# Two query blocks in one stretch of 64x64 tiles, with scores and transposed scores in one PSUM tile

## The chip, the cores and the metric

The kernel runs on one core of one Trainium2 chip. The metric is the device time of one execution in microseconds (us), and less is better. Before the change it is 850.53 us, the median of 3 runs (850.13 to 851.92).

Five engines work side by side, each through a list of its own in order: TensorE (PE, matrix products into PSUM, weights loaded by PEld), VectorE (DVE), ScalarE (ACT), GpSimd (POOL) and SyncE (SP), which here only starts transfers. An engine that meets a wait stands still, and all that is queued behind on it stands still too.

## The reference

```python
B, S, D = 1, 2048, 640;  H = 32; Dh = 20; W = 256;  F = 1536
xn = _layernorm(x)
qkv = (xn @ wqkv).reshape(B, S, 3, H, Dh)            # q, k, v: B H S Dh
scores = einsum("bhqd,bhkd->bhqk", q, k) * Dh ** -0.5
mask = (i - j >= 0) & (i - j < W)                     # i query, j key
p = softmax(where(mask, scores, -1e9))
s = einsum("bhqk,bhkd->bhqd", p, v) -> B S D  @ wo
h = relu(xn @ w1 + b1) ** 2;  g = silu(h @ w2 + b2)
return x + s * g
```

A query sees itself and the 255 keys before it. So a block of 128 queries needs three blocks of 128 keys.

## The kernel before

All big products are made with fp16 operands split into a high and a low part, in three products each (high by high, high by low, low by high).

**Ahead of the loop** the kernel goes through 16 tiles of 128 rows: normalize, turn the tile in five transposes (`tps`, line 256), copy it out as a high part on ACT (line 261) and a low part on DVE (line 266), and multiply by the value weights in two groups of 15 matmuls (`vps`, line 292, by `value_tile`). Each group is taken out of PSUM by ACT (line 305) and twice by DVE (line 307). Before the last four tiles stand eight groups of query and key products (`qkps`, line 503).

**The loop over heads** works on pairs of heads, 16 pairs by 16 blocks of 128 queries, so 256 steps and 13 more to run out. At step s the kernel issues, in order:
- when four blocks are complete, the transpose of their maxima (line 583, into a corner of a score tile), whose rows are copied (`mrow`, line 587) and sent by DMA into the query tile `qs`, where they become extra rows of the contraction;
- the scores of block s (`sps`, line 557): four matmuls of 64 queries by 320 keys, two heads by two halves, in the array's 64x64 tiles;
- ten steps behind (`LAG`), the transposed scores (`stps`, line 604), keys by queries, from which the maxima are now subtracted by the extra rows;
- the maxima of both heads under the mask (line 568, DVE; its accumulator is read out in an instruction of its own), and in every fourth step their split into two fp16 numbers on POOL (`mp`, lines 573 and 574);
- the exponentials (line 609, ACT), and on POOL the two masks (lines 610 and 612);
- a step behind, the high part `ph` of the probabilities on ACT (line 617), and two behind the low part `pl` on DVE (line 623);
- in every second step, the products with the values for two blocks (`ops`, line 637); per four blocks they are copied out (`osb`, line 644), summed and divided (lines 648 to 653) and stored.

Between these, `fill` spreads other products evenly over the steps, the filler: the remaining query and key products (15 matmuls of 512 columns), the MLP's first layer (`hps`, 15 of 256 columns) and its second (`yps`, 36 of 320 columns). Each filler group has its evacuation queued in `pending`, issued by `flush`: for `hps` two ACT passes (`relu`, square), a DVE square and a POOL subtraction, for `yps` one DVE pass (line 886).

**After the loop** comes the output stage: transposes `otp` of the attention's result, groups of 15 matmuls by `wo` (`wops`), and a DVE product and sum per group (lines 983 and 984).

The order on each engine is the order in which the code issues, since the loop stands under `manual_schedule`; the framework adds the waits between instructions that touch the same tile. PSUM has eight banks of 512 fp32 columns. Before, they are separate tiles: three for groups (`pmm`: `vps`, `qkps`, `hps`, `yps`, `wops`), two for scores (`pat`), two in one tile for the transposed scores and `tps` (`pst`), one for the values (`po_`).

Of the kernel before, what the change touches and what calls it, by code (L numbers as in the profile page):

```python
# [34 lines left out]
LAG = 10  # L35
PB = 6
# [3 lines left out]
EARLY_FILL = 0.35  # L40
SWING = 0.3
# [16 lines left out]
def attn_mlp_kernel(ctx: ExitStack, tc, x, wqkv, wo, w1, b1, w2, b2, out):  # L58
# [156 lines left out]
    with tc.tile_pool(name="ph1v", bufs=4) as p1v, tc.tile_pool(name="ph1", bufs=2) as p1, tc.tile_pool(name="ph1x", bufs=4) as p1b, tc.tile_pool(name="ph1w", bufs=1) as p1w:  # L215
        xts, xns, mvs, rstds, turns, vts = {}, {}, {}, {}, {}, {}
        wv = [p1w.tile([P, KC, D], F16, name=f"wv{p}") for p in range(2)]
        sums = po_.tile([P, 64], F32, tag="o", name="sums")
# [28 lines left out]
        def turn(i):  # L247
            if i >= NT:
                return
            b, t = divmod(i, 4)  # L250
            if t == 0:
                xT[b] = big(f"xT_{b}", F16).rearrange("p (s c n) -> p s c n", s=2, c=KC)
            ps = pst.tile([P, 2, 4 * P], F32, tag="st", name="tps").rearrange("p a n -> p (a n)")[:, :D].rearrange("p (c n) -> p c n", n=P)
            xn = xns.pop(i)
            for c in range(KC):
                nc.tensor.transpose(ps[:, c, :], xn[:, c * P:(c + 1) * P], ident)
            turns[i] = (ps, [xT[b][:, part, :, t * P:(t + 1) * P] for part in range(2)])
# [37 lines left out]
        def v_bank(i, nh):  # L295
# [3 lines left out]
            return pmm.tile([P, HALF], F32, tag="mm", name="vps")  # L299
# [33 lines left out]
        with tc.manual_schedule(engines={E_.PE, E_.Activation, E_.DVE, E_.Pool, E_.SP}):  # L333
            warm = p1.tile([P, 1], F32, tag="warm", name="warm")
            nc.scalar.activation(warm, eps, AF.Sqrt)
            warm_ps = pmm.tile([P, P], F32, tag="mm", name="warm_ps")
# [155 lines left out]
            for b in range(NB):  # L492
                for w in "kq":
                    hi, lo = ws0[w]
                    ps = pmm.tile([P, BT], F32, tag="mm", name="qkps")
# [49 lines left out]
    mts = {}  # L545

    def scores(p, q, between):
        i = p % 2
        r = [pat.tile([P, 4 * P], F32, tag="s", name="sps") for h in range(2)]
        rows = between and between(r[0])  # L550
        nk = min(WIN + HB, (q + 1) * P)
        for j in range(2):
            q0 = q * P + j * HB
            k0 = max(0, q0 - WIN)
            for h, ps in enumerate(r):
                rows_ = slice(HB * h, HB * h + HR)
                nc.tensor.matmul(ps[HB * j:HB * (j + 1), :nk], qs[i][rows_, q0:q0 + HB], ks[i][rows_, k0:k0 + nk], start=True, stop=True)  # L557
        return (r, mask if q > 1 else mask0[:, 2 * P - nk:], nk), rows

    def maxima(p, q, r):  # L560
        if q % 4 == 0:
            mts[p, q // 4] = mtp_.tile([P, 8], F32, tag="mt", name="mt")
        mt = mts[p, q // 4]
        r, mk, nk = r
        for h, ps in enumerate(r):
            junk = mtp_.tile([P, WIN + HB], BF16, tag="junk", name="junk")
            at_ = 4 * h + q % 4
            nc.vector.tensor_tensor_reduce(out=junk[:, :nk], in0=ps[:, :nk], in1=mk, scale=1.0 / MAX_UNIT, scalar=-3.0e38, op0=ALU.add, op1=ALU.max, accum_out=mt[:, at_:at_ + 1])  # L568
        if q % 4 == 3:
            mp = mps[q // 4 % 2]  # L570
# [6 lines left out]
    def max_rows(p, g, tp=None):  # L577
        i = p % 2
        mp = mts.pop((p, g))
        if tp is None:  # L580
            tp = pat.tile([P, 4 * P], F32, tag="s", name="mtp")
        tp = tp[:, 3 * P:3 * P + P // 2].bitcast(F16)
# [9 lines left out]
    pts = {}  # L592
    ots = {}
    sts = []

    def scores_t(p, kb):
        i = p % 2
        n = min(3, NT - kb) * P
        ps = sts[0]
        for j in range(2):  # L600
            c0, c1 = HB * j, min(n, WIN + HB * (j + 1))
            for hh in range(2):
                rows_ = slice(HB * hh, HB * hh + ER)
                nc.tensor.matmul(ps[HB * j:HB * (j + 1), hh, c0:c1], ks[i][rows_, kb * P + HB * j:kb * P + HB * (j + 1)], qs[i][rows_, kb * P + c0:kb * P + c1], start=True, stop=True)  # L604
        return ps, n

    def exps(p, kb, ps, n):
        p32 = at2.tile([P, 2, 3 * P], F32, tag="p32", bufs=3, name="p32")
        nc.scalar.activation(p32[:, :, :n], ps[:, :, :n], AF.Exp, scale=esc[0], bias=ebias)  # L609
        nc.gpsimd.affine_select(p32[:, :, 0:P], p32[:, :, 0:P], pattern=[[0, 2], [1, P]], compare_op=ALU.is_ge, fill=0.0, base=0, channel_multiplier=-1)  # L610
        if n == 3 * P:
            nc.gpsimd.affine_select(p32[:, :, 2 * P:], p32[:, :, 2 * P:], pattern=[[0, 2], [-1, P]], compare_op=ALU.is_gt, fill=0.0, base=0, channel_multiplier=1)  # L612
        return p32

    def high(p, kb, p32, n):
        ph = at4.tile([P, 2, 3 * P], F16, tag="ph", name="ph")
        nc.scalar.activation(ph[:, :, :n], p32[:, :, :n], AF.Copy)  # L617
        phs[p, kb] = (ph, p32, n)

    def low(p, kb):  # L620
        ph, p32, n = phs.pop((p, kb))
        pl = at4.tile([P, 2, 3 * P], F16, tag="pl", bufs=PB - 1, name="pl")
        nc.vector.tensor_sub(pl[:, :, :n], p32[:, :, :n], ph[:, :, :n])  # L623
        pts[p, kb] = (ph, pl)

    def values(p, q):
        if q % 4 == 0:
            ots[p, q // 4] = po_.tile([P, 4, 2, VW], F32, tag="o", name="ops")
        ot = ots[p, q // 4]
        vp = vps[p]  # L630
        ksr = list(range(max(0, q - 2), q + 1))
        for hh in range(2):
            m = 0
            for k in ksr:
                for t in pts[p, k]:
                    m += 1
                    nc.tensor.matmul(ot[:, q % 4, hh, :], t[:, hh, (q - k) * P:(q - k + 1) * P], vp[:, k // 4, k % 4, hh, :], start=m == 1, stop=m == 2 * len(ksr))  # L637
        if q >= 2:
            del pts[p, q - 2]

    def normed(p, g):
        ot = ots.pop((p, g))
        osb = at2.tile([P, 8, VW], F32, tag="osb", name="osb")
        nc.scalar.activation(osb, ot.rearrange("p a h w -> p (a h) w"), AF.Copy)

        def rest():
            rs = at2.tile([P, 8], F32, tag="rs", name="rs")
            nc.vector.reciprocal(rs, osb[:, :, VW - 1])
            on = at2.tile([P, 8, DH], F32, tag="on", name="on")
            nc.gpsimd.tensor_add(on, osb[:, :, 0:DH], osb[:, :, DH:2 * DH])  # L650

            def last():
                nc.gpsimd.tensor_mul(on, on, rs.unsqueeze(2).to_broadcast([P, 8, DH]))
                post(o_d[g].rearrange("t p d -> p t d")[:, :, 2 * DH * p:2 * DH * (p + 1)], on.rearrange("p (t h) d -> p t (h d)", t=4))
            norm.append(last)
        return rest


    early = at2.tile([P, 1], F32, tag="early", bufs=1, name="early")
    state = [0.0, 0.0, 0]  # L660
# [10 lines left out]
    pending, late = [], []  # L671
# [5 lines left out]
    def flush(upto=None):  # L677
        for f in late[:]:
            f()
        late.clear()  # L680
        while pending and (upto is None or flushed[0] < upto):
            flushed[0] += 1
            pending.pop(0)()

# [32 lines left out]
    AGE = 2  # L717
# [65 lines left out]
    def second_scales():  # L783
        s2, i2 = weight_scale("w2", totals("w2_t", pmm.tile([P, NF], F32, tag="mm", name="sums2"), mlp["g2"]))
# [220 lines left out]
    with tc.manual_schedule(engines={E_.PE, E_.Activation, E_.DVE, E_.Pool, E_.SP}):  # L1005
# [5 lines left out]
        for s in range(steps):  # L1011
# [30 lines left out]
            if b:  # L1042
                stp = scores_t(*b)
# [56 lines left out]
```

## Time and profile before

| | |
|---|---|
| median of 3 runs | 850.53 us (850.13 to 851.92) |
| the profiled execution | 848.83 us, its span 847.0 us |
| PE busy | 822.7 us, 97% of the span |
| DVE busy | 692.8 us, 82% |
| ACT busy | 648.1 us, 77% |
| POOL busy | 485.0 us, 57% |
| granted TensorE clock, mean | 0.998 |

The span goes from the first to the last instruction of the profiled execution. A busy time is the sum of an engine's instructions; the line that the page gives for a group of instructions has its busy time, the mean of one in ns, and the idle time of the engine just before them with what ended it. The list in order of time gives start, length, engine, line, operation and tile. PE's matmuls run one into the other, so their single lengths overlap their neighbours, and the pitch of a run of them says more than the length of one.

### The profile page before, as it was taken

What the parts mean: (1) busy time and instruction counts of PE and PEld (TensorE: products, weight loads), DVE (VectorE), ACT (ScalarE), POOL (GpSimd) and SP (SyncE); (2) the same over time, 40 slices, a digit from 0 to 9 for tenths busy, and PEclk for the clock granted to TensorE, in tenths of its full rate; (3) what the DMA queues carried; (4) which work ended last, traced back from release to release, by engine and by line L of the source; (5) the groups of instructions that cost most, each with busy time, mean ns of one, the idle gap of its engine ahead of it and who ended that gap; (6) DMA issues with size and microseconds to landing.
All of it is one profiled execution on the core that took longest, in us unless ns stands there. A gap on an engine that the chain in (4) does not pass through costs nothing.

```text
span 847.0 us, 25061 instructions
## 1 busy us (share of the span) xinstructions
PE 822.7 (97%) x9426; PEld 553.4 (65%) x9426; DVE 692.8 (82%) x1897; ACT 648.1 (77%) x1028; POOL 485.0 (57%) x874
## 2 busy tenths in 40 slices
PE   8999998999999999999999999999999999999998
PEld 7765553444444676776766766766767767767775
DVE  6776566788999998898988998888988888975655
ACT  5565446998898997897997997987987988993321
POOL 2000001456665798796896986886986977961000
PEclk9999999999999999999999999999999999999999
DMA  7994349755475311213111222113122113055883
GB/s 245 250 349 129 135 127 283 234 162 157 127 229 163 111 44 55 66 33 89 51 49 50 65 52 65 50 33 84 30 76 65 49 42 99 11 180 171 301 297 126
DMA packets 100498, 104.52 MB, mean 123 GB/s; under 512 B 42520, under 2 KB 72856, under 8 KB 100376
## 3 DMA queue, kind: packets, MB, share of 16 engines
q1 hardware_dynamic: 100376, 102.91, 39.8%
q8 instruction: 74, 1.21, 0.6%
q14 instruction: 48, 0.39, 0.2%
HBM read 65.67 MB, written 36.83 MB: 121 GB/s over the span
## 4 chain that ended last, share of the span: by engine, by line
PE 60%; ACT 14%; POOL 8%; DVE 7%; issue 6%; DMA 3%; SPq 1%; DVEq 0%; ACTq 0%; POOLq 0%
PE yps L882 17%; PE wops L688 8%; PE vps L292 7%; PE hps L688 6%; ACT p L609 5%; PE ops L637 5%; PE qkps L688 5%; PE sps L557 4%; ACT ph L617 3%; PE qkps L503 3%; DVE junk L568 3%; PE stps L604 2%; POOL hh L859 2%; DVE pl L623 2%; ACT relu L855 2%
## 5 line engine op out<-in xcount | busy, mean ns | idle before, releaser
L609 ACT ACTIVATE p<-stps,ebias,esc 128x768 f32<-128x768 f32 (+2 forms) x256 | 242.1, 946 | 59.7 <-PE stps L604 48.9
L568 DVE CUSTOM_DVE_ANT_0 junk<-sps,mask 128x320 bf16<-128x320 f32 (+2 forms) x512 | 220.8, 468 | 49.0 <-PE sps L557 41.4
L623 DVE TENSOR_TENSOR pl<-p,ph 128x768 f16<-128x768 f32 (+2 forms) x256 | 248.8, 972 | 3.8 <-ACT ph L617 3.2
L610 POOL TENSOR_SCALAR_AFFINE_SELECT p<-p 128x256 f32<-128x256 f32 x256 | 163.8, 640 | 86.0 <-ACT p L609 76.7
L617 ACT ACTIVATE ph<-p 128x768 f16<-128x768 f32 (+2 forms) x256 | 203.1, 793 | 2.4 <-POOL p L612 1.6
L688 PE MATMUL hps<-xT,w 128*128 128x256 f16 x1440 | 176.2, 273 | 0.0
L882 PE MATMUL yps<-w,hh 128*128 128x320 f16 x1152 | 174.6, 300 | 0.0
L688 PEld LDWEIGHTS <-w 128*128 128x128 f16 x1440 | 132.6, 98 | 36.0 <-issue 17.2
L882 PEld LDWEIGHTS <-hh 128*128 128x128 f16 x1152 | 104.7, 98 | 57.0 <-issue 18.1
L688 PE MATMUL qkps<-xT,qkw 128*128 128x512 f16 x480 | 115.4, 380 | 0.5 <-DVE w_t L153 0.5
L612 POOL TENSOR_SCALAR_AFFINE_SELECT p<-p 128x256 f32<-128x256 f32 x224 | 103.6, 463 | 0.0
L557 PE MATMUL sps<-ks,qs 60*64 60x320 f16 (+2 forms) x1024 | 87.4, 312 | 6.8 <-DVE mt L568 5.9
L637 PE MATMUL ops<-vp,ph 128*128 128x41 f16 x1440 | 89.8, 181 | 0.0
L637 PE MATMUL ops<-vp,pl 128*128 128x41 f16 x1440 | 89.5, 180 | 0.0
L637 PEld LDWEIGHTS <-ph 128*128 128x128 f16 x1440 | 84.5, 96 | 6.2 <-issue 0.6
L604 PE MATMUL stps<-qs,ks 62*64 62x320 f16 (+4 forms) x1024 | 80.9, 293 | 6.7 <-ACT p L609 6.1
L573 POOL CAST mp<-mt 128x8 f16<-128x8 f32 x64 | 44.6, 698 | 70.0 <-DVE mt L568 69.7
L637 PEld LDWEIGHTS <-pl 128*128 128x128 f16 x1440 | 78.9, 96 | 5.6
L859 POOL TENSOR_TENSOR hh<-sq,hh 128x256 f16<-128x256 f32 x96 | 74.9, 782 | 6.4 <-DVE sq L858 4.3
L688 PEld LDWEIGHTS <-qkw 128*128 128x128 f16 x480 | 41.6, 98 | 55.4 <-issue 11.7
L292 PE MATMUL vps<-wv,xT 128*128 128x320 f16 x480 | 70.3, 303 | 3.2 <-ACT xT L261 1.6
L557 PEld LDWEIGHTS <-qs 60*64 60x64 f16 x1024 | 32.5, 103 | 55.2 <-issue 47.4
(150 smaller groups left out, 1032.4 us busy)
## 6 DMA issues: line engine op xcount, KB each, us to landing
ks<-k_d SPq DMA_DIRECT2D x64, 120.0 KB
qs<-q_d SPq DMA_DIRECT2D x64, 120.0 KB
raw<-in_B_w_dram SPq DMA_DIRECT2D x24, 320.0 KB
v_d<-vt SPq DMA_DIRECT2D x8, 656.0 KB
vp<-v_d SPq DMA_DIRECT2D x16, 328.0 KB
xt<-in_A_x_dram SPq DMA_DIRECT2D x16, 320.0 KB
k_d<-shm SPq DMA_DIRECT2D x20, 256.0 KB
q_d<-shm SPq DMA_DIRECT2D x20, 256.0 KB
```

The costliest lines, as they stand in the source:

```text
L292: nc.tensor.matmul(ps, xT[b][:, xp, c, t * P:(t + 1) * P], wv[wp][:, c, nh * HALF:(nh + 1) * HALF], start=n == 0, stop=n == 3 * KC - 1)
L557: nc.tensor.matmul(ps[HB * j:HB * (j + 1), :nk], qs[i][rows_, q0:q0 + HB], ks[i][rows_, k0:k0 + nk], start=True, stop=True)
L568: nc.vector.tensor_tensor_reduce(out=junk[:, :nk], in0=ps[:, :nk], in1=mk, scale=1.0 / MAX_UNIT, scalar=-3.0e38, op0=ALU.add, op1=ALU.max, ...
L604: nc.tensor.matmul(ps[HB * j:HB * (j + 1), hh, c0:c1], ks[i][rows_, kb * P + HB * j:kb * P + HB * (j + 1)], qs[i][rows_, kb * P + c0:kb * ...
L609: nc.scalar.activation(p32[:, :, :n], ps[:, :, :n], AF.Exp, scale=esc[0], bias=ebias)
L610: nc.gpsimd.affine_select(p32[:, :, 0:P], p32[:, :, 0:P], pattern=[[0, 2], [1, P]], compare_op=ALU.is_ge, fill=0.0, base=0, channel_multip ...
L612: nc.gpsimd.affine_select(p32[:, :, 2 * P:], p32[:, :, 2 * P:], pattern=[[0, 2], [-1, P]], compare_op=ALU.is_gt, fill=0.0, base=0, channel ...
L617: nc.scalar.activation(ph[:, :, :n], p32[:, :, :n], AF.Copy)
L623: nc.vector.tensor_sub(pl[:, :, :n], p32[:, :, :n], ph[:, :, :n])
L637: nc.tensor.matmul(ot[:, q % 4, hh, :], t[:, hh, (q - k) * P:(q - k + 1) * P], vp[:, k // 4, k % 4, hh, :], start=m == 1, stop=m == 2 * le ...
L688: nc.tensor.matmul(ps, a, b_, start=j == 0, stop=j == n - 1)
L882: nc.tensor.matmul(pss[nh], hs[fc][:, hp, tt * P:(tt + 1) * P], lin1(w2t, (2 * fc + wp) * D + nh * HALF, HALF), start=fc == 0 and j == 0, ...
```

## The change

The steps become periods of two query blocks: 128 of them and 8 more. `LAG` is 5 periods, the values come 8 periods behind (`OUT`). In each period one stretch of 64x64 tiles holds the transposed scores of two blocks and then the scores of two blocks. All of them lie in one PSUM tile of six banks, `pair_ps`, three banks for each head: scores at columns 0 and 320, the turned maxima at 640, the transposed scores at 768 and 1152. What crosses a bank's border is cut into two matmuls (`cuts`). The other two banks, `accs`, hold the values of two blocks, or a filler group.

Exponentials are issued per head for two blocks (768 columns, line 628), with the copy of the values (`osb`, line 672) between the two; the masks, the high part (line 643) and the low part (line 650) for two heads and two blocks at once; the maxima (line 581) four a period, first block before second. The four maxima, the split of the maxima and the copy of their rows are issued between stretch and filler.

A filler group's place in PSUM is now chosen by `bank`: one of `accs` when the group won't end within the period, otherwise a bank of `pair_ps`. Ahead of the loop the groups `vps` and `qkps` take turns in three banks of `pair_ps` (`bank3`), and `tps` lies in that tile too; after the loop groups take turns in all eight banks.

The diff, cut to its core:

```diff
-LAG = 10
+LAG = 5
+OUT = LAG + 3
+GUARD = 0.6
+BANK = 512
-    pmm = ctx.enter_context(tc.tile_pool(name="pmm", bufs=3, space=PSUM))
-    pat = ctx.enter_context(tc.tile_pool(name="pat", bufs=2, space=PSUM))
-    pst = ctx.enter_context(tc.tile_pool(name="pst", bufs=1, space=PSUM))
-    po_ = ctx.enter_context(tc.tile_pool(name="po", bufs=1, space=PSUM))
+    psum = ctx.enter_context(tc.tile_pool(name="psum", bufs=1, space=PSUM))
+    pair_ps = psum.tile([P, 2, 3 * BANK], F32, name="pair_ps")
+    accs = [psum.tile([P, BANK], F32, name=f"acc{i}") for i in range(2)]
+    banks = pair_ps.rearrange("p h (a n) -> p (h a) n", n=BANK)
+    turn_ = [0]
+
+    def bank3():
+        turn_[0] += 1
+        return banks[:, 3 + turn_[0] % 3, :]
...
-            return pmm.tile([P, HALF], F32, tag="mm", name="vps")
+            return bank3()[:, 0:HALF]
...
+    def bank(cost, n=BANK):
+
+        if state[2] >= 10 ** 6:
+            rot[0] += 1
+            key = rot[0] % 8
+        elif cost > state[3] - state[0] - GUARD:
+            cross[0] = cross[1]
+            key = cross[0]
+        else:
+            key = (4, 7, 2, 5)[rot[0]] if n <= 2 * P else (2, 5)[rot[0] % 2]
+            rot[0] = (rot[0] + 1) % 4
+        flush(owner.get(key, 0))
+        x = 3 * HB if key in (4, 7) and n <= 2 * P else 0
+        return key, accs[key][:, 0:n] if key < 2 else banks[:, key - 2, x:x + n]
...
-                ps = pmm.tile([P, MT], F32, tag="mm", name="hps")
+                yield (15 * 0.111,)
+                key, ps = bank(15 * 0.111, MT)
...
+        for t in range(periods):
...
+            a, b, c, e = (at(t - lag) for lag in (0, LAG, LAG + 1, OUT))
...
+            flush(max(owner.get(2 + k, 0) for k in range(6)))
+            rot[0] = 0
+            rows = max_rows((t - 2) // (NT // 2), (t - 2) % (NT // 2) // 2) if t % 2 == 0 and 2 <= t <= count else None
+            if b:
+                scores_t(*b)
+            if a:
+                scores(*a)
+            if e:
+                cross[1] = 1 - cross[0]
+                flush(owner.get(cross[1], 0))
+                ot = accs[cross[1]][:, 0:4 * VW].rearrange("p (q h w) -> p q h w", q=2, h=2)
+                values(*e, ot)
+            else:
+                cross[1] = 1 - cross[0]
+            if b:
+                p32s[b] = at2.tile([P, 3 * BANK], F32, tag="p32", bufs=3, name="p32")
+                exps(b[1], p32s[b], 0)
+            norm = taken(*e, ot) if e else None
+            if b:
+                exps(b[1], p32s[b], 1)
+                selects(b[1], p32s[b])
+            if a:
+                for h, q in ((0, 0), (1, 0), (0, 1), (1, 1)):
+                    maxima(a[0], 2 * a[1] + q, h)
+                turned(*a)
+            if rows:
+                rows()
+            if norm:
+                norm()
```

Three places in the engines' lists show what moves. The first is DVE's list in the middle of the loop, before the change: `L568 ISA` is the maximum of a 128x320 score tile, the row after it its accumulator's reading, `pl` the low part; the names in brackets are the engines whose work an instruction waits for.

```order
L568 ISA junk,mt<-sps,mask_102 128x256 [waits DVE_49,PE_49]
L568 ISA mt 128x1
...
L587 COPY mrow<-sps 16x128 [waits DMAHW4_49,DMAHW3_49]
L648 RECIPROCAL rs<-osb 128x8 [waits Activation_49]
L623 TENSOR_TENSOR pl<-p_8001,ph 128x768 [waits Pool_49]
L858 TENSOR_TENSOR sq<-relu 128x256 [waits Activation_49,Pool_49]
L568 ISA junk,mt<-sps,mask 128x320 [waits DVE_49,PE_49]
```

The same place on DVE after the change:

```order
L581 ISA junk,mt<-pair_ps,mask 128x320 [waits DVE_49,PE_49,Activation_49]
L581 ISA mt 128x1
L581 ISA junk,mt<-pair_ps,mask 128x320 [waits DVE_49]
...
L602 COPY mrow<-pair_ps 16x128 [waits DMAHW6_49,DMAHW5_49]
L923 SCALAR_TENSOR_TENSOR ysb<-acc_66,w_i,b2t 128x320 [waits PE_49]
L650 TENSOR_TENSOR pl<-p_8232,ph 128x1536 [waits Activation_49]
...
L680 RECIPROCAL rs<-osb 128x8
```

Two maxima and a low part become four maxima and one low part twice as wide. The first of the four now waits for ACT too; the ACT instruction in question is the second exponential of the same period, which reads other columns of `pair_ps`.

The second place is PE's list around the 64x64 tiles, before the change (`identh,mp` is the transpose of the maxima, `yps` a filler group):

```order
L583 LDWEIGHTS mp_108 [waits Pool_49]
L583 MATMUL sps<-identh,mp_108 128x128 [waits DVE_49]
L557 LDWEIGHTS qs_126
L557 MATMUL sps<-ks_127,qs_126 64x256
...
L604 LDWEIGHTS ks_1563
L604 MATMUL stps<-qs_1562,ks_1563 64x320 [waits Activation_49]
...
L882 LDWEIGHTS hh
L882 MATMUL yps<-w_0_3695,hh 128x320
```

After the change:

```order
L732 MATMUL acc_66<-xT_725,w_2_1404 128x256
L598 LDWEIGHTS mp_101 [waits DVE_49,Pool_49]
L598 MATMUL pair_ps<-identh,mp_101 128x128 [waits Activation_49]
L620 LDWEIGHTS ks_121
L620 MATMUL pair_ps<-qs_120,ks_121 64x256
...
L570 MATMUL pair_ps<-ks_1499,qs_1498 64x320
...
L663 MATMUL acc_65<-vp_9551,ph 128x41 [waits Activation_49]
...
L732 LDWEIGHTS w_0_1266 [waits DVE_49]
L732 MATMUL pair_ps<-xT_725,w_0_1266 128x256 [waits Activation_49]
```

Transposed scores now stand ahead of scores, two blocks of each, and the values follow them. The transpose ahead of the stretch waits for DVE, POOL and ACT, and so does, by its weights and its first matmul, a filler group (`hps`) that lies in `pair_ps`.

The third place is PE's list ahead of the loop, before the change (`vps` the value products of a tile of rows, `tps` the transposes of the next):

```order
L292 MATMUL vps<-wv_146,xT_756 128x320
L292 LDWEIGHTS xT_756 [waits DVE_49,Activation_49]
L292 MATMUL vps<-wv_146,xT_756 128x320 [waits PE_49]
...
L256 MATMUL tps<-ident,xn 128x128 [waits PE_49]
L256 MATMUL tps<-ident,xn 128x128 x4
L292 LDWEIGHTS xT_756
```

After the change:

```order
L298 LDWEIGHTS xT_725 [waits DVE_49,Activation_49]
L298 MATMUL pair_ps<-wv_140,xT_725 128x320 [waits Activation_49]
...
L262 MATMUL pair_ps<-ident,xn 128x128 [waits DVE_49,Activation_49]
L262 MATMUL pair_ps<-ident,xn 128x128 x4
L298 LDWEIGHTS xT_725
L298 MATMUL pair_ps<-wv_140,xT_725 128x320 [waits DVE_49]
```

The order of the products is the same. What is new are the waits at the head of each group and of the transposes: they name the copies out of the group or the transposes just before.

More of the change, by code (lines that the diff above doesn't have):

```diff
@@ L545, in attn_mlp_kernel @@
     mts = {}
-    def scores(p, q, between):
-        i = p % 2
[L549 to L558, printed above, removed]
@@ L615, in high @@
[L615 to L639, printed above, removed]
@@ new lines, in values @@
+    def values(p, v, ot):
+        vp = vps[p]
+        for q in (2 * v, 2 * v + 1):
+            ksr = list(range(max(0, q - 2), q + 1))
+            for hh in range(2):
+                m = 0
+                for k in ksr:
+                    x = 3 * P * (2 * hh + k % 2) + (q - k) * P
+                    for t in pts[p, k // 2]:
+                        m += 1
+                        nc.tensor.matmul(ot[:, q % 2, hh, :], t[:, x:x + P], vp[:, k // 4, k % 4, hh, :], start=m == 1, stop=m == 2 * len(ksr))
+        pts.pop((p, v - 1), None)
+        if v == NT // 2 - 1:
+            del pts[p, v]
@@ L970, in out_filler @@
                     sl = slice(nh * HALF, (nh + 1) * HALF)
-                    ps = pmm.tile([P, HALF], F32, tag="mm", name="wops")
+                    yield (15 * 0.138,)
+                    key, ps = bank(15 * 0.138, HALF)
                     mms = []
```

286 lines of the change are left out of this document (150 added, 136 removed).

## The prediction

> **What bounds the kernel now.** I read the page first, then the busy time by stretches, then one piece of the loop in order of time.
>
> ```profile
> PE 822.7 (97%) x9426; PEld 553.4 (65%) x9426; DVE 692.8 (82%) x1897; ACT 648.1 (77%) x1028; POOL 485.0 (57%) x874
> ```
>
> TensorE (PE) is busy 97% of the span. The windows before, in and after the loop over heads (busy us of PE, weight loads, VectorE (DVE), ScalarE (ACT), GpSimd (POOL)) give the three lengths that I sum against:
>
> ```profile
> 0.00:118.70 118.70, 113.92 (x798) 78.18 (x798) 80.84 (x204) 65.17 (x135) 7.20 (x37) 0.99 0.66 209
> 118.70:763.00 644.30, 629.42 (x7993) 415.37 (x7993) 562.55 (x1602) 560.36 (x858) 475.33 (x834) 1.00 0.33 94
> 763.00:847.00 84.00, 79.33 (x638) 59.80 (x636) 49.44 (x94) 22.58 (x36) 2.44 (x4) 1.00 0.66 225
> ```
>
> The loop takes 644.3 us for 269 steps, and PE is idle for 15 us of it. Two steps look like this (start, length, engine, line, operation, count; in brackets the idle time before and who ended it):
>
> ```profile
> 449.20 0.49 DVE L568 CUSTOM_DVE_ANT_0 junk<-sps,mask 128x320 bf16<-128x320 f32 x1 [0.55 <-PE sps L557]
> 449.22 2.08 PE L882 MATMUL yps<-w,hh 128*128 128x320 f16 x14
> 449.34 0.99 ACT L609 ACTIVATE p<-stps,ebias,esc 128x768 f32<-128x768 f32 x1 [0.56 <-PE stps L604]
> 450.02 0.08 DVE L568 DVE_READ_ACCUMULATOR2_ANT mt<- 128x1 f32 x1
> 450.02 0.95 DVE L623 TENSOR_TENSOR pl<-p,ph 128x768 f16<-128x768 f32 x1
> 450.17 0.85 POOL L573 CAST mp<-mt 128x8 f16<-128x8 f32 x1 [0.90 <-DVE mt L568]
> 450.23 0.83 ACT L617 ACTIVATE ph<-p 128x768 f16<-128x768 f32 x1
> 451.11 0.20 POOL L574 TENSOR_TENSOR mp<-mt,mp 128x8 f16<-128x8 f32 x1
> 451.23 0.33 PE L557 MATMUL sps<-ks,qs 60*64 60x320 f16 x4
> 451.39 0.27 PE L604 MATMUL stps<-qs,ks 62*64 62x256 f16 x4
> 451.59 1.40 PE L882 MATMUL yps<-w,hh 128*128 128x320 f16 x9
> 453.44 0.22 PE L583 MATMUL sps<-identh,mp 128*128 128x128 f16 x1
> 453.58 0.33 PE L557 MATMUL sps<-ks,qs 60*64 60x320 f16 x4
> 453.74 0.22 PE L604 MATMUL stps<-qs,ks 62*64 62x128 f16 x4
> 453.90 2.08 PE L882 MATMUL yps<-w,hh 128*128 128x320 f16 x14
> 455.04 0.21 DVE L587 COPY mrow<-sps 16x128 f16<-16x128 f16 x1
> 455.17 0.18 DVE L648 RECIPROCAL rs<-osb 128x8 f32<-128x8 f32 x1
> ```
>
> PE goes from one matmul to the next without waiting, and the other engines work beside it: the maxima (L568) run at the same time as the exponentials (L609), on different PSUM tiles. Two steps take 4.68 us (449.22 to 453.90).
>
> **What the change gives.** Fourteen matmuls take 2.08 and nine 1.40, a pitch of 0.136, so the first run would hand over at 451.12, and the way into the 64x64 tiles costs 0.1. A set of four 320-column matmuls takes 0.16 (451.23 to 451.39), and the way out about 0.08 more (0.20 for a 256-column set). Two visits cost 2 x (0.1 + 0.16 + 0.24) = 1.0. The one stretch streams the same columns in six sets, since three pieces are cut at bank borders: an estimate of 0.70, with its ways in and out 0.88. That saves 0.12 us a period, over 128 periods 15 us, if PE goes on setting the pace: 4.56 us a period.
>
> **What it adds: waits on the whole of one PSUM tile.** Scores, turned maxima and transposed scores now lie in one tile of six banks, and the order of the changed program shows what that did. The exponentials wait for the last score matmul, though the transposed scores come first. The first maximum waits for ACT as well, and what ACT must have finished there is the second exponential, since both read the tile. The next period's first 64x64 matmul, and any filler group placed in the tile, wait for all of these. Queued behind the waiting maximum on DVE are three more maxima, the copies out of PSUM and the low parts pl; behind the waiting matmul on PE stands everything, since PE takes its list in order. So the period has a chain, with S the start of the stretch and about 0.07 for a hop (the accumulator read ends at 450.10, the CAST starts at 450.17):
>
> ```profile
> L609 ACT ACTIVATE p<-stps,ebias,esc 128x768 f32<-128x768 f32 x224 | 220.7, 985 | 55.1 <-PE stps L604 45.2 <-DVE pl L623 7.0 <-DVE ysb L886 1.5
> L644 ACT ACTIVATE osb<-ops 128x328 f32<-128x328 f32 x64 | 27.8, 434 | 5.7 <-PE ops L637 5.5
> L573 POOL CAST mp<-mt x64: 189/854/922, 126.2 to 739.0; 128x8 f16<-128x8 f32 x64
> L574 POOL TENSOR_TENSOR mp<-mt,mp x64: 201/204/722, 126.5 to 740.0; 128x8 f16<-128x8 f32 x64
> 485.74 0.71 PE L688 MATMUL hps<-xT,w 128*128 128x256 f16 x5
> 487.39 2.03 PE L688 MATMUL hps<-xT,w 128*128 128x256 f16 x17
> 453.30 1.00 DVE L886 SCALAR_TENSOR_TENSOR ysb<-yps,w_i,b2t 128x320 f32<-128x320 f32 x2
> ```
>
> Scores end at S + 0.85 and the first exponential starts at 0.92. It hands over after 0.89 (449.34 to 450.23), a half-size osb copy takes 0.2 (estimate: half the columns of 0.434), the second exponential 0.985: 3.0. Four maxima at 0.41 (two in 449.20 to 450.02): 4.71. That is more than PE's 4.56 before anything follows. Four kinds of period follow, counted in the order of the changed program:
>
> - Even, no filler in the tile (37): copy 0.21, hop and first weights 0.15: 5.1 us.
> - Odd (39): the turned maxima are now needed at the very next stretch, where before they had two steps' time. CAST at 4.86, free 0.19, then the subtraction; with weights and the transpose (0.14, 453.44 to 453.58) the next stretch starts at 5.7. But the traced CAST took 0.85, until pl ended, and 0.854 is the median: POOL stands still under pl. Where pl follows the reciprocal directly it starts at 4.82, takes 1.75 (estimate: twice 0.95 less one start), and the period is 7.2. Free, with a shm copy ahead of pl, are 10; bare or with a SBUF square ahead 16 (the square is taken to block too); with a ysb copy ahead, 0.5 long, 13, where it is a toss-up: 6.5.
> - A 256-column filler group in the tile (44): it can't start before 5.0, takes 15 x 0.11 = 1.65 (pitch (2.03 - 0.71)/12), and in the order 1.33 on average of the next group, in another tile, follow it: 8.15.
> - The first 9 and last 7 periods, without values or scores: 4.3, near PE's pace.
>
> Loop: 44 x 8.15 + 37 x 5.1 - 5 (short first blocks) + 10 x 5.7 + 13 x 6.5 + 16 x 7.2 + 69 = 869, which is +225 us. The switch saving is inside these chains and no longer seen. With every toss-up free it is +214, with everything blocked +244.
>
> The same tile serves the stage ahead of the loop, where three banks turned before:
>
> ```profile
> 26.27 4.08 PE vps L292 x30
> 30.89 4.08 PE vps L292 x30
> 73.21 3.24 PE qkps L503 x15
> 102.48 16.30 PE vps L292 x120
> L292 PE MATMUL vps<-wv,xT 128*128 128x320 f16 x480 | 70.3, 303 | 3.2 <-ACT xT L261 1.6 <-ACT wv L371 1.5
> L305 ACT ACTIVATE vt<-vps 128x320 f16<-128x320 f32 x32 | 14.0, 441 | 8.8 <-PE vps L292 8.5
> L307 DVE SCALAR_TENSOR_TENSOR vt<-vps,vt 128x160 f16<-128x160 f32 x64 | 17.7, 320 | 17.0 <-ACT vt L305 16.8
> L261 ACT ACTIVATE xT<-tps 128x640 f16<-128x640 f32 x16 | 11.0, 689 | 4.7 <-PE tps L256 4.7
> L266 DVE TENSOR_TENSOR xT<-tps,xT 128x640 f16<-128x640 f32 x16 | 13.1, 817 | 7.3 <-ACT xT L261 7.3
> ```
>
> Each group (14 x 0.136 + 0.303 = 2.2) must now be taken out by ACT (0.441) and DVE (2 x 0.32) before the next starts: 3.5 with hops. The transposes between (4.62 - 4.08 = 0.54, with their tail 0.7) and their two copies (0.689, 0.817) stand in line too: 2.4. A tile of 4.62 becomes 9.4: 11 tiles, +53. The eight qk groups (3.24) gain about 1.4 each, and three transposes 1 each: +14. The last eight groups (16.30/8 = 2.04) go to 3.5: +12. The first tile: +3. Sum +82.
>
> After the loop, groups turn over eight banks of which six are this tile. In the order 28 of 56 groups stop after their first matmul until the copy of the group two places back is done.
>
> ```profile
> L983 DVE SCALAR_TENSOR_TENSOR res<-wops,o_inv,yb 128x320 f32<-128x320 f32 x32 | 17.6, 550 | 24.2 <-PE wops L688 20.0 <-DMA out_dram<-res 4.2
> ```
>
> That is 0.85 with tail and hops for 16 of them, about 1.5 for 12 transposes with two copies: +32; if half is covered +15.
>
> The other edits I cost at nothing: one ACT and one DVE split of 1536 columns in place of two of 768, two masks over four blocks, two osb copies a group in place of one, other lags. They lie beside the chain; if that cover were gone, the wide ones save a start each, 0.2 us a period. The DMAs on SP's queue are the same, and rows that a stretch waits for are posted three periods ahead.
>
> **The clock.** The granted clock, the third number from the end of a window's row, is 1.00 nearly everywhere. Once it was halved, right after a window in which PE was busy 1.86 of 3.41 us:
>
> ```profile
> 10.24:13.65 3.41, 1.86 (x13) 1.27 (x13) 3.08 (x9) 2.65 (x6) 1.35 (x5) 1.00 0.89 300
> 13.65:17.07 3.42, 3.42 (x16) 2.36 (x15) 3.42 (x6) 2.20 (x4) 0.00 (x0) 0.51 0.82 294
> ```
>
> The 44 periods of 8.15 leave PE idle some 2.7 us in one piece, and so do the 16 blocked ones and the tiles ahead of the loop. If half of the 71 are followed by a 3.4 us window at half speed, which costs 1.4 us of work: +50. Bounds: 0, and 130 if nearly all are and the halved work falls on the chain.
> [...]
>
> **Sum.** 847.0 + 225 + 82 + 32 + 50 = 1236 as a span. The profiled execution took 848.83, 1.8 more than its span, and the median is 850.53: **1240 us**. What a measurement of this kernel can tell from no change is about 0.2%.
>
> **Rivals.**
> - *Forecast, waits on the whole tile and some windows at half clock*, 1150 to 1300: 0.58. For it: the waits are in the program.
> - *The clock falls nearly every time*: 50 becomes 130 to 180, 1300 to 1370: 0.17. For it: the one halved window; against: a single case.
> - *The chains are partly covered*: if groups in the tile wait 1.5 us less, because fewer hops count, the odd periods are all free and the clock stays: 1240 - 66 - 30 - 50 = 1094, 1030 to 1150: 0.20.
> - *Not slower*: the waits name work that is done by then, because the maxima run beside the exponentials as at 449.34. It decides at the first maximum: within 0.3 us of the last score matmul, the chain is 0.92 + 4 x 0.41 + 0.36 = 2.9 and PE's 4.56 rules: 850.5 - 15 = 835. Against it: the wait on ACT in the order. 0.03, with 0.01 for no change and 0.01 for a still slower case.
> [...]
>
> Faster 0.03, same 0.01, slower 0.96. The range 1080 to 1340 takes in nearly all of the forecast's own, the upper half of the covered case and the lower half of the clock's, 0.8 in all.
>
> **Right or wrong.** In the profile after, DVE's first maximum should sit idle until ACT's exponential, not PE, ends it; PE's largest idle groups should be the filler in the tile and the 64x64 matmuls, released by DVE, ACT and POOL; the stage ahead of the loop should reach to 200 us; PEclk should show digits under 9. Maxima that start beside the first exponential, or a loop period near 4.6 us, would prove me wrong.

## The result and the profile after

The changed kernel takes **1244.49 us** (median of 4 runs, 1238.94 to 1248.01) against 850.33 before (median of 4 runs): 1.463 times as long (95% interval 1.456 to 1.470). The forecast was 1240 us, within 1080 to 1340. The profiled execution spans 1245.9 us.

From the page after, the busy times and the clock in 40 slices:

```profile
PE 922.6 (74%) x10386; PEld 614.1 (49%) x10386; DVE 662.5 (53%) x1785; ACT 656.9 (53%) x1012; POOL 413.9 (33%) x634
PEclk9767699999989889989889789889888898798899
```

PE has fallen from 97% to 74% of the span. It is busy 100 us longer than before: the same products, cut into more matmuls, and some of them at half clock (the mean granted clock is 0.893, before 0.998). No other engine has taken PE's place; DVE and ACT stand at 53%. The same stretches as in the prediction, after (busy us of PE, weight loads, DVE, ACT, POOL, then the granted clock); the first four rows are the start, the value tiles, the query and key groups and the last value tiles ahead of the loop, then come the loop up to the output stage's first transposes, and the rest:

```profile
0.00:13.65 13.65, 10.53 (x65) 9.90 (x66) 6.13 (x15) 8.57 (x18) 4.29 (x25) 1.00 0.84 293
13.65:153.50 139.85, 89.17 (x418) 50.33 (x415) 49.21 (x133) 39.34 (x85) 1.33 (x5) 0.73 0.33 105
153.50:202.00 48.50, 35.44 (x196) 16.71 (x197) 15.94 (x35) 11.03 (x17) 1.56 (x7) 0.89 0.31 92
202.00:230.70 28.70, 18.06 (x123) 11.19 (x121) 13.38 (x25) 11.64 (x18) 0.00 (x0) 1.00 0.26 84
230.70:1122.40 891.70, 683.01 (x9028) 467.74 (x9029) 530.68 (x1490) 563.53 (x843) 406.53 (x597) 0.91 0.23 68
1122.40:1245.90 123.50, 86.43 (x562) 58.27 (x560) 47.20 (x89) 22.84 (x33) 0.18 (x1) 0.92 0.45 153
```

The same marks of the kernel before:

```profile
13.65:73.00 59.35, 57.68 (x416) 41.42 (x415) 43.66 (x124) 32.41 (x80) 1.34 (x5) 0.97 0.75 235
73.00:102.30 29.30, 29.30 (x199) 15.20 (x198) 18.81 (x43) 13.46 (x23) 1.56 (x7) 1.00 0.56 175
102.30:118.70 16.40, 16.40 (x121) 11.64 (x119) 12.00 (x23) 10.50 (x16) 0.00 (x0) 1.00 0.35 105
118.70:767.40 648.70, 633.82 (x8045) 418.70 (x8045) 564.98 (x1605) 561.09 (x859) 476.78 (x835) 1.00 0.33 94
767.40:847.00 79.60, 74.93 (x586) 56.47 (x584) 47.01 (x90) 21.85 (x34) 0.99 (x2) 1.00 0.68 233
```

So 112 us came ahead of the loop (118.7 to 230.7), 243 in it (648.7 to 891.7) and 44 after it (79.6 to 123.5): together the 399 by which the span grew.

What the engines waited for, after (total us, times, longest):

```profile
DVE junk L581 <- ACT p L628: 189.3, 115, 5.1
ACT p L628 <- PE pair_ps L570: 176.5, 107, 7.8
PE pair_ps L732 <- DVE mrow L602: 66.0, 22, 3.4
PE pair_ps L732 <- DVE mt L581: 65.7, 21, 4.1
PE pair_ps L598 <- POOL mp L591: 39.2, 35, 3.5
PE pair_ps L298 <- DVE xT L272: 20.8, 12, 2.6
PE pair_ps L298 <- DVE vt L313: 20.4, 16, 2.3
```

The first maximum now waits until ACT releases it, where it was PE before, and PE waits for maxima, for the copy of their rows, for POOL, and ahead of the loop for the copies out of the tile. One period in order of time, followed by the next stretch:

```profile
489.39 0.47 PE L620 MATMUL pair_ps<-qs,ks 62*64 62x256 f16 x12 [0.41 <-DVE mrow L602]
489.69 0.44 PE L570 MATMUL pair_ps<-ks,qs 60*64 60x320 f16 x12
490.24 0.99 ACT L628 ACTIVATE p<-pair_ps,ebias,esc 128x768 f32<-128x768 f32 x1 [1.42 <-PE pair_ps L570]
491.13 0.30 ACT L672 ACTIVATE osb<-acc 128x164 f32<-128x164 f32 x1
491.31 0.99 ACT L628 ACTIVATE p<-pair_ps,ebias,esc 128x768 f32<-128x768 f32 x1
492.34 0.49 DVE L581 CUSTOM_DVE_ANT_0 junk<-pair_ps,mask 128x320 bf16<-128x320 f32 x1 [1.34 <-ACT p L628]
493.58 0.49 DVE L581 CUSTOM_DVE_ANT_0 junk<-pair_ps,mask 128x320 bf16<-128x320 f32 x1
494.21 0.19 POOL L590 CAST mp<-mt 128x8 f16<-128x8 f32 x1 [0.61 <-DVE rs L680]
494.48 0.20 POOL L591 TENSOR_TENSOR mp<-mt,mp 128x8 f16<-128x8 f32 x1
494.74 0.23 PE L598 MATMUL pair_ps<-identh,mp 128*128 128x128 f16 x1
```

From the stretch's start (489.39) the first exponential comes after 0.85 us, the first maximum after 2.95, the last one's end after 4.7, and the next stretch after 5.35. The scores that the first maximum reads were complete at 490.13 at the latest; it starts 2.2 us after that, at the end of an exponential that reads other columns and writes none of the tile. In all of the 123 periods that have both, the first maximum starts behind the second exponential's end.

The trace gives the granted clock in windows of 3.41 us. Ahead of the 44 filler groups that lie in the tile in the loop, PE stands still for 1.8 to 4.1 us (median 3.2), and 36 of these 44 periods have a window at half clock; here is the longest of these gaps, 4.1 us:

```profile
645.72:649.13 3.41, 0.00 (x0) 0.00 (x0) 3.17 (x8) 3.19 (x4) 3.32 (x4) 1.00 0.00 1
649.13:652.55 3.42, 3.19 (x16) 2.26 (x17) 0.29 (x3) 0.00 (x0) 1.15 (x4) 0.51 0.16 29
```

In the first window PE ran nothing. In the second its group of 15 matmuls, released by the last maximum, took 3.33 us, where it takes 1.8 at full clock.

### The profile page after: what moved, and what is told of

Its sections match the earlier page's. It is cut to its first block, busy times and chain, and to the rows that moved or that the text cites. A ratio compares the mean times of both kernels' runs of the same rounds, so it can differ in the third digit from the quotient of the medians.

```text
span 1245.9 us, 26252 instructions
## 1 busy us (share of the span) xinstructions
PE 922.6 (74%) x10386; PEld 614.1 (49%) x10386; DVE 662.5 (53%) x1785; ACT 656.9 (53%) x1012; POOL 413.9 (33%) x634
## 5 line engine op out<-in xcount | busy, mean ns | idle before, releaser
L628 ACT ACTIVATE p<-pair_ps,ebias,esc 128x768 f32<-128x768 f32 (+2 forms) x288 | 250.9, 885 | 179.4 <-PE pair_ps L570 176.5
L581 DVE CUSTOM_DVE_ANT_0 junk<-pair_ps,mask 128x320 bf16<-128x320 f32 (+2 forms) x512 | 212.1, 470 | 193.1 <-ACT p L628 189.3
L732 PE MATMUL pair_ps<-xT,w 128*128 128x256 f16 x660 | 121.5, 361 | 134.8 <-DVE mrow L602 66.0
L650 DVE TENSOR_TENSOR pl<-p,ph 128x1536 f16<-128x1536 f32 x144 | 217.9, 1522 | 2.6 <-ACT ph L643 2.2
L643 ACT ACTIVATE ph<-p 128x1536 f16<-128x1536 f32 x144 | 181.0, 1269 | 0.5 <-POOL p L634 0.5
L732 PE MATMUL acc<-w,hh 128*128 128x320 f16 x1152 | 169.9, 303 | 7.7 <-ACT osb L672 7.7
L298 PE MATMUL pair_ps<-wv,xT 128*128 128x320 f16 x480 | 99.2, 377 | 46.3 <-DVE xT L272 20.8
L732 PE MATMUL acc<-xT,qkw 128*128 128x512 f16 x480 | 115.2, 391 | 6.2 <-ACT osb L672 6.2
L732 PE MATMUL acc<-xT,w 128*128 128x256 f16 x780 | 117.1, 307 | 0.0
L663 PE MATMUL acc<-vp,ph 128*128 128x41 f16 x1440 | 91.0, 182 | 4.9 <-DVE shm L87 3.5
```

Of the source, the lines that this page charges most:

```text
L298: nc.tensor.matmul(ps, xT[b][:, xp, c, t * P:(t + 1) * P], wv[wp][:, c, nh * HALF:(nh + 1) * HALF], start=n == 0, stop=n == 3 * KC - 1)
L581: nc.vector.tensor_tensor_reduce(out=junk[:, :nk], in0=pair_ps[:, h, o:o + nk], in1=mk, scale=1.0 / MAX_UNIT, scalar=-3.0e38, op0=ALU.add, ...
L628: nc.scalar.activation(dst, src, AF.Exp, scale=esc[0], bias=ebias)
L643: nc.scalar.activation(h_, s_, AF.Copy)
L650: nc.vector.tensor_sub(l_, s_, h_)
L663: nc.tensor.matmul(ot[:, q % 2, hh, :], t[:, x:x + P], vp[:, k // 4, k % 4, hh, :], start=m == 1, stop=m == 2 * len(ksr))
```

## The experiments

The theory: accesses to the one tile wait for each other, whatever banks they touch, and these waits also bring windows at half clock. The rivals: the new order by itself (wide exponentials, then four maxima) makes the chain; the clock falls for another reason; groups wait for their evacuation in any bank. None of the kernels leaves out work. Times are medians, ratios are against the kernel before.

**Own tiles ahead of the loop.** The three pools of the old layout serve that stage and are given up before the six-bank tile is made.

```diff
+    with tc.tile_pool(name="pmm", bufs=3, space=PSUM) as pmm, tc.tile_pool(name="pst", bufs=1, space=PSUM) as pst, tc.tile_pool(name="po", bufs=1, space=PSUM) as po_, ...
-            ps = pair_ps[:, 0, :D].rearrange("p (c n) -> p c n", n=P)
+            ps = pst.tile([P, 2, 4 * P], F32, tag="st", name="tps")...
-            return bank3()[:, 0:HALF]
+            return pmm.tile([P, HALF], F32, tag="mm", name="vps")
```

> Only the stage ahead of the loop gets PSUM tiles of its own again (three for groups, one of two banks for the transposes), given up before the six-bank tile is made. Theory (waits on the whole tile, and half-clock windows that follow from them): the stage goes from 230.7 us back to about 119 at a clock of 1.00, the loop stays at 892 us, 1244.5 - 112 = 1132 us, 1122 to 1142. Rival (the evacuations by ACT and DVE set the stage's pace in any layout, and only the slow clock is a loss): about 24 us return, 1220.

Measured: 1141.35 us, ratio 1.341 (1.337 to 1.345). The same windows of this kernel:

```profile
0.00:119.90 119.90, 113.82 (x802) 78.15 (x803) 81.49 (x206) 66.48 (x137) 7.22 (x37) 0.99 0.65 207
119.90:1015.80 895.90, 686.81 (x9029) 469.96 (x9030) 530.42 (x1490) 564.27 (x843) 407.76 (x597) 0.90 0.23 68
1015.80:1138.90 123.10, 86.35 (x561) 58.08 (x559) 47.17 (x89) 22.85 (x33) 0.12 (x1) 0.92 0.45 153
```

The stage is back at 119.9 and the other two have hardly moved (895.9 and 123.1). So 111 of its 112 us hung on the tiles; the rival's 1220 falls.

**Dummy work ahead of the loop.** In the changed kernel, three times per tile of rows:

```diff
+            warm_up(8 * ahead)
             v_products(ps, i, 0, V_TERMS)
+            warm_up(8 * ahead)
...
+            warm_up(8 * ahead)
             v_products(ps, i, 1, V_TERMS)
```

> Work is added: ahead of the loop, in each of 11 tiles of rows, three times 8 transposes of the identity (0.109 us each at full clock, 0.87 a time, 29 us in all) into a free bank, just before an instruction that waits; their results aren't used. Theory (windows in which PE is busy less than half are followed by windows at half clock): PE stays busy, the clock stays at 1.00, the stretch from 13.65 to 153.5 us, which is 24 longer than the sum of the waits alone, loses about those 24: 1220 us, 1212 to 1232. Rival (the clock has another cause, or the added work stands in line): unchanged 1244, up to 29 more, 1273.

Measured: 1217.34 us, 27 less than without the added work, ratio 1.432 (1.426 to 1.437). The stretch in question and the stage as a whole:

```profile
13.65:130.00 116.35, 94.19 (x695) 72.35 (x694) 50.86 (x137) 40.68 (x88) 1.34 (x5) 0.99 0.41 131
...
0.00:203.30 203.30, 154.35 (x1066) 108.39 (x1070) 84.62 (x206) 70.44 (x137) 7.20 (x37) 0.97 0.39 125
```

With PE kept busy the clock stays at 0.99 instead of 0.73, and the stage takes 203.3 us. So of its 112 us at least 27 were clock, and at most 84.6 waits, since the added work itself may have cost a little.

**Filler outside the tile.** In the changed kernel:

```diff
-        elif cost > state[3] - state[0] - GUARD:
-            cross[0] = cross[1]
-            key = cross[0]
         else:
-            key = (4, 7, 2, 5)[rot[0]] if n <= 2 * P else (2, 5)[rot[0] % 2]
-            rot[0] = (rot[0] + 1) % 4
+            cross[0] = 1 - cross[0]
+            key = cross[0]
```

> The loop's filler groups take turns in the two banks outside the six-bank tile, none is put into the tile. Theory (43 of the periods are long, 9.25 us, because their filler in the tile waits for all four maxima): these come down to about the 5.3 of the others, 43 x 3.95 = 170 us less, 1075 us, 1050 to 1105. Rival (a group waits for evacuations in any bank, since ACT's list is full of exponentials and high parts): periods of about 7, 1150. If the filler's place doesn't matter: 1244.

Measured: 1094.80 us, ratio 1.289 (1.285 to 1.292). The loop's window:

```profile
227.60:977.60 750.00, 633.95 (x9028) 443.43 (x9029) 536.80 (x1490) 558.80 (x843) 415.14 (x597) 0.97 0.27 80
```

The loop loses 142 of the 170 us that were expected, and the clock rises from 0.91 to 0.97. Even periods now take 5.3 us on average and odd ones 6.1. Ten of the 119 counted still have a window at half clock; the others take 5.1 and 5.8, little more than the 5.0 and 5.7 that periods without such groups had before. Part of what the rival expected is in the difference, since PE's waits for the copy of the values before a filler group rise from 14 to 36 us.

**Two tiles by head.** The same six banks, as two tiles:

```diff
-    pair_ps = psum.tile([P, 2, 3 * BANK], F32, name="pair_ps")
+    pair_ps = [psum.tile([P, 3 * BANK], F32, name=f"pair{h}") for h in range(2)]
...
-                for h, q in ((0, 0), (1, 0), (0, 1), (1, 1)):
+                for h, q in ((0, 0), (0, 1), (1, 0), (1, 1)):
```

> The six-bank tile becomes two tiles of three banks, one for each head, at the same addresses and with the same work; the maxima of the first head go ahead of those of the second. Theory (reads of other banks of the same tile wait for each other): the first maximum waits for the first exponential instead of the second, the chain of a period falls by about 1, filler in the first head's tile may start after two maxima; periods of 6.1 with filler in the tile, 4.6 even, 4.8 odd: loop 892 - 187 = 705, ahead of the loop 15 less (transposes and groups in different tiles), 1042 us, 1000 to 1090. Rival (the wide exponentials followed by four maxima are the chain by themselves, as the program's order has it, and tiles don't matter): 1244, within 2%.

Measured: 1070.85 us, ratio 1.259 (1.257 to 1.262). The wait of the maxima for the exponentials, and the three windows:

```profile
DVE junk L581 <- ACT p L628: 102.0, 137, 3.6
```

```profile
0.00:169.60 169.60, 120.93 (x803) 77.60 (x804) 83.15 (x206) 69.93 (x137) 7.20 (x37) 0.97 0.47 150
169.60:971.70 802.10, 653.18 (x9027) 453.65 (x9028) 544.93 (x1491) 562.06 (x843) 405.99 (x597) 0.94 0.26 75
971.70:1069.20 97.50, 76.65 (x562) 55.62 (x560) 46.73 (x89) 22.64 (x33) 0.17 (x1) 0.99 0.56 193
```

That wait falls from 189.3 to 102.0 us, with the same instructions. The total is within the range, but the parts were sized wrongly: ahead of the loop 61 us went instead of 15, since transposes and groups in different tiles also keep the clock up (0.97), and in the loop 90 instead of 187. There the clock has a share: periods with filler in a tile take the 6.1 us that were expected where the clock stays full, but 18 of the 43 have a window at half clock and take 9.3.

**Only the order of the maxima**, in the one tile (the last edit above alone).

> One tile as in the changed kernel, and only the order of the four maxima is altered: both of the first head, then both of the second. Theory (the one tile makes the first maximum wait for the second exponential whatever its order): 1244 us, within 0.5%. Rival (the order of the maxima gave the two tiles by head their gain): 1071.

Measured: 1240.31 us, ratio 1.459 (1.457 to 1.461), its loop 888.3 us. So the order gave the last kernel next to nothing; its gain came from the tiles.

**The parts together**, first with filler in the tiles by head, then without it. After the loop, groups take turns in four separate tiles.

```diff
-            key = rot[0] % 8
+            key = (0, 2, 1, 5)[rot[0] % 4]
```

> Three undone parts together: own tiles ahead of the loop, the two tiles by head, and after the loop groups take turns in four separate tiles (two single banks, one bank of each head's tile). Filler is still put into the heads' tiles. Theory (the parts add up, since each takes away waits at its own place): 119.9 us ahead of the loop, the 802 of the two tiles by head, about 85 after it, 1007 as a span, 1009 us, 990 to 1025. Rival (they share the half-clock windows, so that the gains overlap or grow): below 980 or above 1040.

> The same, and filler only in the two banks outside. Theory: no period is left with filler waiting in a score tile; even periods 4.6 (the first head's maxima beside the second exponential, PE's own 4.56), odd 5.1: loop 675, 120 ahead, 90 behind, 885 us, 860 to 920, within a few per cent of the 850 before the change. Rival (two banks for values and filler make each group wait for its evacuation behind the exponentials, as the 5.7 of odd periods with filler outside the one tile might be read): loop 740, 950.

Measured: 1003.70 us, ratio 1.181 (1.180 to 1.183), as expected; and 933.97, ratio 1.099 (1.097 to 1.102), 14 us outside its range. The output stage of the second, 79.2 us at clock 0.99, is what it was before the change (79.6):

```profile
120.00:849.90 729.90, 625.79 (x9029) 441.21 (x9030) 547.88 (x1491) 556.72 (x843) 410.78 (x597) 0.98 0.28 83
849.90:929.10 79.20, 74.49 (x561) 55.69 (x559) 47.05 (x89) 21.74 (x33) 0.10 (x1) 0.99 0.68 238
```

and what its PE still waits for in the loop:

```profile
PE pair L593 <- POOL mp L586: 45.0, 40, 2.4
PE acc L724 <- ACT osb L667: 39.2, 62, 1.7
```

The transpose of the maxima (L593) waits for POOL, and filler for the copy of the values: odd periods take 5.9 us on average, not 5.1, and even ones 5.1, not 4.6. The next three kernels take these two waits.

**The transpose behind the scores.**

```diff
-            rows = max_rows(...) if t % 2 == 0 and 2 <= t <= count else None
             if b:
                 scores_t(*b)
             if a:
                 scores(*a)
+            rows = max_rows(...) if t % 2 == 0 and 2 <= t <= count else None
...
                     maxima(a[0], 2 * a[1] + q, h)
+                    if rows and (h, q) == (0, 1):
+                        rows()
+                        rows = None
```

> The same as the one before, and the transpose of the maxima stands behind the scores of its stretch instead of ahead of the transposed scores; the copy of its rows stands behind the first head's maxima. Theory (odd periods are longer because the stretch's first instruction waits for the maxima's split on POOL): the odd periods come to the length of the even ones, 64 x 0.5 = 32 us less than the kernel before it, about 850 us. Rival (the odd periods wait for evacuations or for DVE's list): no difference to the kernel before it, within 5 us.

Measured: 910.99 us, ratio 1.072 (1.071 to 1.074), 23 less instead of 32. The odd periods come down from 5.9 to 5.3 us on average, but the even ones go up from 5.1 to 5.4.

**Another bank for the first group.**

```diff
-            cross[0] = 1 - cross[0]
+            if not fresh[0]:
+                cross[0] = 1 - cross[0]
+            fresh[0] = False
             key = cross[0]
...
-            flush(max(owner.get(2 + k, 0) for k in range(6)))
+            flush()
+            fresh[0] = bool(held_)
```

> The 911 us kernel (own tiles ahead, two tiles by head, filler outside, the transpose behind the scores) with one rule more: where no filler group goes on over a period's border, the first group of the period takes the bank of the last group, which has been taken out during the stretch, and not the bank of the values. Theory (of the 63 us that its loop is longer than before the change, some 43 are waits of the first filler group for the copy of the values, which stands between the two exponentials in ACT's list): about half to two thirds of these go, 885 us, 875 to 897. Rival (the group then waits for its own bank's evacuation, or the time is lost at the next stretch): 905 to 920.

Measured: 901.45 us, ratio 1.060 (1.059 to 1.062), 10 less: between theory and rival, inside neither range. The waits of the kernel before it and, below, its own:

```profile
PE acc L724 <- ACT osb L667: 42.5, 62, 1.9
PE pair L593 <- POOL mp L586: 18.7, 23, 1.9
...
PE pair L593 <- POOL mp L586: 30.5, 31, 2.2
PE acc L726 <- ACT osb L667: 19.6, 35, 2.3
```

The waits for the copy lost 23 us, and the transpose, which comes earlier now, waits 12 more for POOL: the second half of the rival.

**The transpose behind the values, in the second head's tile.**

```diff
-        tp = pair_ps[0][:, TURNED_AT:TURNED_AT + P // 2].bitcast(F16)
+        tp = pair_ps[1][:, TURNED_AT:TURNED_AT + P // 2].bitcast(F16)
...
             else:
                 cross[1] = 1 - cross[0]
+            rows = max_rows(...) if t % 2 == 0 and 2 <= t <= count else None
...
                     maxima(a[0], 2 * a[1] + q, h)
-                    if rows and (h, q) == (0, 1):
-                        rows()
-                        rows = None
```

The copy of the rows goes back behind all four maxima with it, which the expectation doesn't name.

> The same, and the transpose of the maxima stands behind the values, in the tile of the second head, whose exponential starts later anyway. Theory (19.7 us are waits of the transpose for POOL): 15 to 20 less than the one before, 868 us, 855 to 885, near the 850 before the change. Rival (the second exponential waits for the transpose in its place): no difference to the one before, within 5 us.

Measured: 880.32 us, ratio 1.036 (1.035 to 1.038), 21 less, just over the 15 to 20 expected. The transpose's waits for POOL fall from 30.5 to 13.3 us; what share the copy's new place has in the gain is not separated. That wait, and the loop:

```profile
PE pair L593 <- POOL mp L586: 13.3, 16, 1.5
...
120.00:801.90 681.90, 622.67 (x9029) 441.44 (x9030) 544.93 (x1491) 555.80 (x843) 413.18 (x597) 0.98 0.30 89
```

With these edits 364 of the 394 us are back, and the two-block periods are still 30 us behind the kernel before. What remains is in the loop: PE is busy 11 us less than before (622.7 against 633.8) but idle for 59 us instead of 15. No version here beats the kernel before.

## Why the prediction was right, and where its sizes were off

**The mechanism is shown.** The steps that the prediction named stand in the trace at their places: exponentials behind the last score matmul, the first maximum behind the second exponential (2.95 us after the stretch's start, forecast 3.0 to 3.07), next stretch and filler behind the maxima. Splitting the tile, with work and banks unchanged, took 174 us off; the order alone took 4, which is inside the spread of the runs; own tiles ahead of the loop took 103; four tiles after it brought the output stage back to 79.2. The waits stood between reads in different banks too (the first maximum started 2.2 us after its scores, behind an exponential that reads other columns), and the kernel with two tiles did without those between the two heads.

**The total was closer than its terms, by luck.** Three sizes were off, and their errors cancelled: the odd periods and the filler in the tile were 67 us too dear, the clock some 65 too cheap.

| term | forecast | measured |
|---|---|---|
| waits ahead of the loop | 82 | 84.6, with the clock held up |
| even periods, 37 | 5.1 each | 5.0 each |
| odd periods, 39 | 5.7, 6.5 or 7.2, on average 6.58 | 5.71 on average at full clock |
| periods with filler in the tile, 44 | 8.15 each | 7.4 each at full clock |
| half-clock windows | 50 | about 115 |
| after the loop | 32 | 44, with clock 0.92 |

*The odd periods* failed at one step: how often, and for how long, "POOL stands still under pl". The row of the CAST after:

```profile
L590 POOL CAST mp<-mt 128x8 f16<-128x8 f32 x64 | 21.1, 329 | 86.7 <-DVE mt L581 54.0 <-DVE rs L680 32.7
```

Its mean is 0.33 us. It mostly starts some 0.02 us behind the reciprocal's end, when DVE is already in its next instruction. Beside a `ysb` or `shm` copy it took 0.19 us (the toss-up came out free), beside a square 0.33 or less, until that square's end and not until the low part's. Only in nine of 64 did the low part follow at once: it took 1.66 in two, as feared, and 0.59 in the seven whose low part is cut in two. So the odd periods came out 34 us below the forecast (39 periods by 6.58 - 5.71). A slip beside it: from the prediction's own counts, everything blocked gives +249, not +244.

*The periods with filler in the tile* start their group after 4.7 us rather than 5.0, and less comes behind it than the forecast put there; the 8 of them that saw no half-clock window lasted 7.4 us. That is 44 x 0.75 = 33 us less.

*The clock* cost more. The other 36 such periods lasted 9.7 us on average, 2.3 more, together some 82; 4 more fell on other periods of the loop, 27 ahead of it, and a few after the loop, where the clock was 0.92. The 115 are an estimate from these. The forecast let half of the long waits be followed by a slow window. In fact four in five of these periods had one, so the rival in which the clock falls nearly every time (130 to 180) was nearer on the clock, while the chains came out shorter than forecast. The gaps, put at some 2.7 us, were longer too: a median of 3.2 ahead of the filler in the tile, and four of PE's gaps in the loop were longer than 3.41 us, up to 4.1. The clock fell 55 times in the trace, so these four explain few of them.

**The two rivals on the faster side.** No maximum started beside the first exponential, so 835 stayed out of reach; the covered chains were right on the odd periods (34 us for its 30), half right on the filler in the tile (33 for its 66), and wrong on the full clock that they were to bring. The saving from one stretch for two was forecast at 15 us of PE's time; the 880 us kernel, in which PE is hardly slowed, shows 11.

**Open.** The 30 us by which the best of these kernels stays behind aren't split up further. Running the transpose of the maxima a whole period later was not tried. Nor was another layout: the second block's scores (columns 320 to 639) reach into the bank in which the transposed scores begin (column 768, with the kernel's 512 columns a bank), so within a head part of the remaining waits may be between accesses to one bank. No run separates these from the waits between banks.

## What to carry to other kernels

Look at which instructions of the changed program wait for which before timing it: here one PSUM tile over several banks made even reads in different banks take turns (in all of the 123 periods the first maximum stood behind the second exponential), and a chain of exponentials and maxima that had run side by side became the period. Split such a tile along a line that no instruction crosses (here the heads, 174 us less), and keep what can fill a gap in tiles of its own (150 less). Price a chain of waits together with the clock that it brings: here 50 of the 56 full-speed windows in which TensorE was busy under half were followed by one at half clock.

## What the runs showed of the hardware

In the trace of the changed kernel the granted clock followed how busy PE had been in the window of 3.41 us before. Counted by the matmul records: of full-speed windows with PE busy under 40%, all 41 were followed by one at half clock; between 40 and 50%, 9 of 15; between 50 and 60%, 5 of 31; from 60% on none of 199. A half-clock window with PE busy 80% or more was followed by full clock (all 55), one below that by another at half clock (all 22). In the kernel before, one of 3 full-speed windows between 50 and 60% was followed by half clock, and none of 241 from 60% on. So between 40 and 60% the same busy share was followed by either clock; no run was made to find a border.

No single long gap was needed. In the stretch from 13.65 to 153.5 us, where the mean clock was 0.73, PE's longest gap was 2.6 us, less than one window. Here work that wasn't needed paid: 264 dummy transposes, 29 us by the pitch of 0.109 of those that warm PE up in the kernel before (20 in 2.18 us), made the kernel 27 us faster, with the clock of that stretch at 0.99.
